# Three edits in an attention, expert and gated-unit kernel: no zeroing of x2, splits moved in the queues, a narrower low product

## The chip, the cores and the metric

The kernel runs on one core of one Trainium2 chip. The metric is device time in microseconds. The kernel before took 451.92 us (median of three runs, 451.65 to 452.31). The engines are TensorE (PE, with its weight load PEld), VectorE (DVE), ScalarE (ACT), GpSimd (POOL) and SyncE (SP, which issues most DMAs).

## The reference, cut to what matters

Three parts follow on each other. A linear attention with a decayed state runs over 768 tokens of 2 batches and 8 heads of 48, which gives 1536 tokens of 384 values. A layer of eight experts sends each token to the one with the highest gate value. A gated unit follows:

```
h   = maximum(disp @ w1, 0)          # per expert, 384 -> 1024
y   = h @ w2                         # 1024 -> 384
x   = gate_w * y, back in the tokens' order
out = (silu(x @ w_gate) * (x @ w_val)) @ w_out   # 384 -> 1536 -> 384
```

All is in float32. The kernel reaches that precision with fp32r matmuls, by splitting each operand in a high and a low part (the cast to fp32r, and what the cast left over) and adding three products: high by high, high by low, low by high.

## The kernel before, in words

The attention takes the first 77 us. It is not touched. Its last step gives the experts' inputs: the rows of x lie in DRAM sorted by expert, each expert's block has room for 224 tokens (BLK), and x2 (three tiles of 128 rows by 1536 + 224 columns, in SBUF) takes the experts' results, one column for each token in the order of the experts.

**An expert** (`experts`, loop over e, then over f from 0 to 15) has an up phase (f below 8) and a down phase. In the up phase each f does nine matmuls of 224 columns (line 857): for each of three slices k of the input the high weights by the high part of x, by its low part, and the low weights by the high part. The first expert uses plain float32 there (line 869). `relu` then makes the high part (ScalarE, 876) and the low part (VectorE, 877) of the hidden values, side by side in one tile of 448 columns, high in the first 224 (HI) and low in the others (LO). In the down phase each f does three calls of `product`, one for each k: the high weights by all 448 columns (line 846), and the low weights by the first columns (line 847). `store` adds the two halves of the result and writes them to x2 at the expert's place (896, 897). Several experts' blocks overlap in x2: each writes 224 columns from its first token on, and the next one writes over what was too much.

Beside this the loop splits weights for later (`feed`: a cast on ScalarE, line 713, and a subtraction on VectorE, 714), loads weights (703), turns the next expert's rows by TensorE (838), and splits them in the high part (`x_part`: ScalarE, 729) and the low part (VectorE, 730), one k for each f behind the turn. In the first expert the turn is at f = 11, the parts at f = 12 to 14; four memsets at f = 8 to 11 (1020) zero x2's first 1536 columns, 384 at a time, between the first expert's weight splits.

**The gated unit** (`gated`) works on four groups g of 384 tokens, and on six chunks c of 256 hidden values, of which the first three go chunk by chunk over all groups. `inner(c, g)` has two steps f; each does 18 matmuls of 384 columns (gate and value, lines 1072 to 1074), then Silu on ScalarE (1076), the product on VectorE (1077), the cast of the high part on ScalarE (1080) and the subtraction on GpSimd (1081). `outer` does the last product (1094 to 1096) for the group before. `x2_split` splits x2 for one group and one k (ScalarE 1044, VectorE 1045). Groups 0 and 1 are split while the last expert runs; the six splits of groups 2 and 3 are in the list `later`, of which one is taken in each of the first six steps. `background` does a step of the conversion of the gated unit's weights in between (790 to 823).

Nothing is scheduled by a planner: the order within each engine's queue is that in which the code issues the instructions, each engine takes its queue in order, and semaphores hold an instruction until its inputs are there and its output's buffer is free.

Of the kernel before, what the change touches and what calls it, by code (L numbers as in the profile page):

```python
# [41 lines left out]
HI, LO = slice(0, BLK), slice(BLK, 2 * BLK)  # L42
# [10 lines left out]
TG = 384  # L53
# [16 lines left out]
class Kernel:  # L70
# [772 lines left out]
    def product(self, ps, wh, wl, xc, first, last):  # L843

        nc = self.nc
        nc.tensor.matmul(ps[:, 0:2 * BLK], lhsT=wh, rhs=xc, start=first, stop=False, skip_group_check=True)  # L846
        nc.tensor.matmul(ps[:, 0:256], lhsT=wl, rhs=xc[:, 0:256], start=False, stop=last, skip_group_check=True)  # L847

    def up(self, f, x):

# [78 lines left out]
    def experts(self, st):  # L929
        tc, nc, a, cp = self.tc, self.nc, self.a, self.cp  # L930
        hpool = self.ep = self.pool(st, "ep", side="right")
        self.ps_y = self.pool(st, "ps_y", space=PSUM)
        self.ps_x = self.pool(st, "ps_x", space=PSUM)
        x2 = self.x2

        NU = 8
        by_f = [(f, k) for f in range(NF) for k in range(KD)]
        by_k = by_f[0:KD * NF // 2] + [(f, k) for k in range(KD) for f in range(NF // 2, NF)]


        counts = self.counts
        offs = self.offs = cp.tile([P, E], F32, name="offs")
        self.by_expert = cp.tile([P, NT], I32, name="by_expert")
        offs_i = cp.tile([1, 2, E], I32, name="offs_i")
        rare = cp.tile([P, 2], F32, name="rare")
        rare_i = self.rare_i = cp.tile([1, 1], I32, name="rare_i")

        def order():
            self.order()
            nc.vector.tensor_copy(offs_i[:, 0], offs[0:1])  # L950
            for e in range(1, E):
                nc.vector.tensor_scalar(
                    out=offs_i[:, 1, e:e + 1], in0=counts[0:1, e:e + 1], scalar1=float(e * ST), scalar2=None, op0=ALU.add
                )

            nc.vector.tensor_reduce(rare[:, 0:1], counts, AX.X, ALU.max)
            nc.vector.tensor_scalar(out=rare[:, 0:1], in0=rare[:, 0:1], scalar1=float(BLK), scalar2=None, op0=ALU.is_gt)
            nc.vector.scalar_tensor_tensor(
                out=rare_i, in0=self.bad[0:1], scalar=float(HP * (P - 2 * D)), in1=rare[0:1, 0:1],
                op0=ALU.is_gt, op1=ALU.add,  # L960
            )


        n_loaded, n_split = RAWS, 1

        def feed(used):

            nonlocal n_split
            if n_split < min(max(used - 4, 0) + WS, E * NU - 4):
                self.unit_split((n_split + 4) % NU)  # L970
                n_split += 1

        def load(n, used, eng=None):
            nonlocal n_loaded
            for _ in range(n):

                o = n_loaded - RAWS
                if n_loaded < E * NU and (o < used if o < 4 else o - 4 < n_split):
                    self.unit_load(n_loaded // NU, n_loaded % NU, eng)
                    n_loaded += 1  # L980

        x = self.x0
        last, xrs = None, {}
        for e in range(E):
            hc, py = self.tiles()
            for f in range(2 * NF):
                if f < NF:
                    ph = self.up(f, x) if e else self.up_plain(f, x)
                else:

                    i = (f - NF) * KD
                    self.down((by_f if e + 1 < E else by_k)[i:i + KD], py, hc)
                if e == 0 and f == 1:
                    xrs[1] = self.x_block(ST)
                if f == (5 if e == 0 else 1):
                    if e == 0:
                        self.places()
                    if e + 2 < E:

                        end = nc.values_load(  # L1000
                            offs_i[0:1, 1, e + 2:e + 3], engines=[ET.SP], min_val=(e + 2) * ST, max_val=(e + 2) * ST + N
                        )
                        self.clear_rows(self.x_disp[ds(end, BLK)])
                    if e == 0:
                        self.background(1, 2)
                if e == 1 and f < NT:
                    self.place_id(f)
                turn = NF + 2 if e else NF + 3
                if f == turn and e + 1 < E:
                    x = self.new_x(self.x_turn(xrs[e + 1]))  # L1010
                if turn < f <= turn + KD and e + 1 < E:
                    self.x_part(x, f - turn - 1)
                if f % 2:
                    feed(e * NU + f // 2)

                load(2, e * NU + (f + 1) // 2, nc.scalar if e == 0 and f < 4 else None)
                if f == NF + 5 and e + 2 < E:
                    xrs[e + 2] = self.x_block((e + 2) * ST)
                if e == 0 and f in range(8, 12):
                    nc.vector.memset(x2[:, :, (f - 8) * TG:(f - 7) * TG], 0.0)  # L1020
                if f in ((12, 14) if 0 < e < E - 3 else (10, 12, 14) if 0 < e < E - 1 else ()):
                    self.background(1, 2)
                if f < NF:
                    self.relu(f, ph, hc)
                if e == 0 and f == 3:
                    order()
                if last and f in (0, 2, 4):
                    self.store(*last, f // 2)
                if e == E - 1 and NF <= f < NF + 2 * KD:
                    self.x2_split((f - NF) // KD, [(f - NF) % KD])  # L1030
                if e == E - 1 and f >= 2 * NF - KD:
                    self.store(py, self.place(offs_i[0:1, 0, e:e + 1], ET.DVE), f - (2 * NF - KD))
            for q in range(0 if e else 4, NU):
                self.units[q].pop(0)
            if e < E - 1:
                last = py, self.place(offs_i[0:1, 0, e:e + 1], ET.DVE)
# [10 lines left out]
    def gated(self, st, at_end=lambda: None):  # L1047
        nc, a = self.nc, self.a
# [10 lines left out]
        later = []  # L1059

        def inner(c, g, steps, limit):

            parts = []
            xh, xl = self.x2s[g]
            for f in range(2):
                pg = {}
                fs = slice(f * P, (f + 1) * P)
                for m in ("w_gate", "w_val"):
                    wh, wl = self.wff[c % 3][m]
                    pg[m] = (pg2.tile([P, 512], F32, name="g2", tag="g2") if f else self.pa_tile())[:, 0:TG]  # L1070
                    for k in range(KD):
                        nc.tensor.matmul(pg[m], lhsT=wh[:, k, fs], rhs=xh[:, k], start=(k == 0), stop=False)
                        nc.tensor.matmul(pg[m], lhsT=wh[:, k, fs], rhs=xl[:, k], start=False, stop=False)
                        nc.tensor.matmul(pg[m], lhsT=wl[:, k, fs], rhs=xh[:, k], start=False, stop=(k == KD - 1))  # L1074
                sg = wk.tile([P, TG], F32, name="sg", tag="sg", bufs=3)
                nc.scalar.activation(sg, pg["w_gate"], AF.Silu)  # L1076
                nc.vector.tensor_mul(sg, pg["w_val"], sg)  # L1077
                h_ = wk.tile([P, TG], F32R, name="ah", tag="ah", bufs=8)
                l_ = wk.tile([P, TG], F32R, name="al", tag="al", bufs=8)
                nc.scalar.copy(h_, sg)  # L1080
                nc.gpsimd.tensor_sub(l_, sg, h_.bitcast(F32))  # L1081
                parts.append((h_, l_))
                if later:
                    self.x2_split(*later.pop(0))
                self.background(steps, *limit)
            return [(c, f, *parts[f]) for f in range(2)]

# [27 lines left out]
        for c in range(HALF):  # L1115
            for g in range(NG):

                limit = (c + 3, True) if g else (c + 2, False)
                parts = inner(c, g, 2 if c else 1, limit)
                if before:  # L1120
                    outer(*before, False, 1, limit)
                before = g, parts, c == 0
# [157 lines left out]
```

## Time and profile before

| | |
|---|---|
| median of three runs | 451.92 us (451.65 to 452.31) |
| profiled execution | 451.35 us |
| its span, first to last instruction | 449.7 us |
| TensorE busy | 430.9 us (96%) |
| VectorE, ScalarE, GpSimd busy | 293.5, 213.2, 156.6 us |
| mean granted TensorE clock | 0.989 of full speed |
| experts | about 77 to 213 us |
| gated unit | about 213 to 440 us |

The profile is of one execution. A row of the timeline gives the start and the duration in microseconds, the engine, the line, the operation and the tiles it writes and reads; in brackets stands how long the engine had been idle just before, and which instruction ended that. Matmuls overlap in the pipeline, so what one of them costs is read from the distance of two starts, not from its duration. Weight loads run beside the matmuls.

### The profile page before, as it was taken

To read this page: it belongs to the slowest core of one execution; us is meant where nothing else is said; L and a number is where in the kernel's file an instruction comes from. 1 tells how busy PE (TensorE), PEld (TensorE's weight loads), DVE (VectorE), ACT (ScalarE), POOL (GpSimd) and SP (SyncE) were. 2 spreads that over 40 slices of the span, in tenths; PEclk is the share of its full clock that TensorE was granted. 3 is DMA by queue.
4 is the path that set the end of the run, shared out by engine and by line. 5 is a ranking of instruction groups with operands and counts; after the bars stand their busy time and mean duration, and the time that the engine had idled before them with its cause. 6 is when DMAs were issued, how large, how long until landed. Compare 5 with 4: busy or idle time off the path is not lost. (4 is left out here: it accounts for less than half of the span.)

```text
span 449.7 us, 8371 instructions
## 1 busy us (share of the span) xinstructions
PE 430.9 (96%) x3179; PEld 417.5 (93%) x3179; DVE 293.5 (65%) x576; ACT 213.2 (47%) x471; POOL 156.6 (35%) x147
## 2 busy tenths in 40 slices
PE   8889989999999999999999999999999999999991
PEld 7778778989999999999998999999999999999991
DVE  6999985886887977986557788978865111111110
ACT  2688864636756756755555534353343031230310
POOL 5846543102111110000343556454546233332321
PEclk9999999989999999999999999999999999999996
DMA  7999932698999999602022423233200100101001
GB/s 260 355 303 354 404 107 78 204 369 251 265 224 254 279 261 256 231 1 72 0 71 70 136 85 133 79 133 111 101 1 1 52 1 17 37 0 54 1 20 41
DMA packets 24819, 63.78 MB, mean 142 GB/s; under 512 B 4801, under 2 KB 10049, under 8 KB 24769
## 3 DMA queue, kind: packets, MB, share of 16 engines
q1 hardware_dynamic: 22128, 57.43, 40.1%
q0 software_dynamic: 1920, 4.73, 2.9%
q10 hardware_dynamic: 720, 1.00, 0.8%
q8 instruction: 27, 0.44, 0.4%
q14 instruction: 24, 0.19, 0.1%
HBM read 55.67 MB, written 7.48 MB: 140 GB/s over the span
## 5 line engine op out<-in xcount | busy, mean ns | idle before, releaser
L1081 POOL TENSOR_TENSOR al<-sg,ah 128x384 fp32r<-128x384 f32 x48 | 54.2, 1128 | 135.2 <-ACT ah L1080 135.2
L714 DVE TENSOR_TENSOR wlo<-raw,whi 128x768 fp32r<-128x768 f32 x60 | 57.3, 954 | 9.3 <-ACT whi L713 9.1
L846 PE MATMUL py<-hc,whi 128*128 128x448 f32 x192 | 63.1, 370 | 0.0
L1080 ACT CAST ah<-sg 128x384 fp32r<-128x384 f32 x48 | 24.7, 515 | 78.2 <-DVE sg L1077 78.2
L857 PE MATMUL A<-xc,whi 128*128 128x224 f32 x336 | 59.2, 280 | 1.0 <-DVE xc L730 0.9
L857 PEld LDWEIGHTS A<-xc,whi 128*128 128x128 f32 x336 | 52.5, 196 | 1.9 <-DVE xc L730 1.5
L847 PE MATMUL py<-hc,wlo 128*128 128x256 f32 x192 | 53.8, 280 | 0.0
L713 ACT CAST whi<-raw 128x768 fp32r<-128x768 f32 x60 | 49.8, 837 | 0.7 <-PE py L846 0.7
L1094 PE MATMUL po<-w_out_hi,ah 128*128 128x384 f32 x144 | 48.6, 337 | 0.0
L1096 PE MATMUL po<-w_out_hi,al 128*128 128x384 f32 x144 | 48.5, 337 | 0.0
L1095 PE MATMUL po<-w_out_lo,ah 128*128 128x384 f32 x144 | 48.5, 337 | 0.0
L857 PE MATMUL A<-xc,wlo 128*128 128x224 f32 x168 | 46.9, 279 | 0.0
L924 POOL DMA_INDIRECT ids<-tok,by_expert x12 | 13.7, 1145 | 75.6 <-DMA ids<-tok,by_expert 67.2
L1103 DVE TENSOR_TENSOR acc<-acc,po 128x384 f32<-128x384 f32 x36 | 19.3, 547 | 30.9 <-PE po L1096 30.9
L846 PEld LDWEIGHTS py<-hc,whi 128*128 128x128 f32 x192 | 36.1, 188 | 2.5
L1077 DVE TENSOR_TENSOR sg<-A,sg 128x384 f32<-128x384 f32 x24 | 13.3, 555 | 38.0 <-PE A L1074 30.3
L847 PEld LDWEIGHTS py<-hc,wlo 128*128 128x128 f32 x192 | 36.5, 190 | 0.0
L1077 DVE TENSOR_TENSOR sg<-g,sg 128x384 f32<-128x384 f32 x24 | 13.3, 555 | 34.5 <-PE g L1074 27.6
L876 ACT ACTIVATE hc<-A 128x224 fp32r<-128x224 f32 x64 | 23.1, 362 | 22.8 <-PE A L857 20.0
L276 ACT ACTIVATE AT<-ident,c 128x128 f32<-128x128 f32 x96 | 29.4, 389 | 9.6 <-DVE c L263 9.6
L857 PEld LDWEIGHTS A<-xc,wlo 128*128 128x128 f32 x168 | 33.1, 197 | 0.0
L1076 ACT ACTIVATE sg<-A 128x384 f32<-128x384 f32 x24 | 11.6, 485 | 34.7 <-PE A L1074 34.7
(169 smaller groups left out, 1100.7 us busy)
## 6 DMA issues: line engine op xcount, KB each, us to landing
raw<-in_w SPq DMA_DIRECT2D x62, 384.0 KB, 6.8
rkT<-in_rkT SPq DMA_DIRECT2D x12, 512.0 KB, 6.5
rk<-in_rk SPq DMA_DIRECT2D x12, 384.0 KB, 4.7
raw<-in_w_gate SPq DMA_DIRECT2D x6, 768.0 KB, 4.2
raw<-in_w_val SPq DMA_DIRECT2D x6, 768.0 KB, 4.1
raw<-in_w_out SPq DMA_DIRECT2D x6, 768.0 KB, 4.3
x_disp<-zero SPq DMA_DIRECT2D x8, 336.0 KB, 8.1
xr<-x_disp SPq DMA_DIRECT2D x8, 336.0 KB, 6.1
```

The lines of the kernel that those rows point to most:

```text
L276: nc.scalar.activation(AT[i][:, j, hp], ident, AF.Copy, scale=cc[i][:, j, hp:hp + 1])
L713: nc.scalar.copy(h_, raw)
L714: nc.vector.tensor_sub(l_, raw, h_.bitcast(F32))
L846: nc.tensor.matmul(ps[:, 0:2 * BLK], lhsT=wh, rhs=xc, start=first, stop=False, skip_group_check=True)
L847: nc.tensor.matmul(ps[:, 0:256], lhsT=wl, rhs=xc[:, 0:256], start=False, stop=last, skip_group_check=True)
L857: self.nc.tensor.matmul(ph[:, HI], lhsT=w[:, k, fs], rhs=x[1][:, k, half], start=(k == 0 and i == 0), stop=(k == KD - 1 and i == 2),)
L1077: nc.vector.tensor_mul(sg, pg["w_val"], sg)
L1080: nc.scalar.copy(h_, sg)
L1081: nc.gpsimd.tensor_sub(l_, sg, h_.bitcast(F32))
L1094: nc.tensor.matmul(po, lhsT=ah[:, ts_], rhs=wh, start=(i == 0), stop=False)
L1095: nc.tensor.matmul(po, lhsT=ah[:, ts_], rhs=wl, start=False, stop=False)
L1096: nc.tensor.matmul(po, lhsT=al[:, ts_], rhs=wh, start=False, stop=(i == len(parts) - 1))
```

## The change

x2 is no longer zeroed. In the gated unit a step's split from the list `later` is issued ahead of the step's matmuls, where it was issued behind the step's casts. In the experts' down product the low weights take the 224 columns of the high part, where they took 256 (the last 32 of these were columns of the low part).

```diff
@@ product
         nc.tensor.matmul(ps[:, 0:2 * BLK], lhsT=wh, rhs=xc, start=first, stop=False, skip_group_check=True)
-        nc.tensor.matmul(ps[:, 0:256], lhsT=wl, rhs=xc[:, 0:256], start=False, stop=last, skip_group_check=True)
+        nc.tensor.matmul(ps[:, HI], lhsT=wl, rhs=xc[:, HI], start=False, stop=last, skip_group_check=True)
@@ experts
                     xrs[e + 2] = self.x_block((e + 2) * ST)
-                if e == 0 and f in range(8, 12):
-                    nc.vector.memset(x2[:, :, (f - 8) * TG:(f - 7) * TG], 0.0)
                 if f in ((12, 14) if 0 < e < E - 3 else (10, 12, 14) if 0 < e < E - 1 else ()):
@@ gated, inner
             for f in range(2):
                 pg = {}
+                if later:
+                    self.x2_split(*later.pop(0))
                 fs = slice(f * P, (f + 1) * P)
...
                 parts.append((h_, l_))
-                if later:
-                    self.x2_split(*later.pop(0))
                 self.background(steps, *limit)
```

## Rows read from the trace of the kernel before

**Rows 1.** The page: TensorE's busy time; its granted clock in 40 slices.
```profile
PE 430.9 (96%) x3179; PEld 417.5 (93%) x3179; DVE 293.5 (65%) x576; ACT 213.2 (47%) x471; POOL 156.6 (35%) x147
...
PEclk9999999989999999999999999999999999999996
```

**Rows 2.** Windows: stretch, length, busy PE, PEld, DVE, ACT, POOL, clock, DMA share, GB/s.
```profile
95.00:98.00 3.00, 2.01 (x10) 1.19 (x9) 2.25 (x6) 2.06 (x4) 0.45 (x1) 1.00 1.00 371
98.00:101.40 3.40, 3.40 (x17) 3.40 (x18) 2.70 (x5) 1.68 (x4) 0.00 (x0) 0.50 1.03 365
...
115.00:204.00 89.00, 89.00 (x697) 87.28 (x696) 75.52 (x136) 57.74 (x126) 9.01 (x8) 1.00 0.77 221
```

**Rows 3.** Timeline of VectorE, 88 to 98 us: start, duration, instruction, idle before.
```profile
94.14 1.02 DVE L1020 MEMSET x<- 128x1152 f32 x1 [0.19 <-issue]
95.07 0.33 DVE L730 TENSOR_TENSOR xc<-px,xc 128x224 fp32r<-128x224 f32 x1
...
97.42 0.38 DVE L730 TENSOR_TENSOR xc<-px,xc 128x224 fp32r<-128x224 f32 x1
```

**Rows 4.** Timeline of TensorE, 97 to 110 us.
```profile
97.86 0.45 PE L857 MATMUL A<-xc,whi 128*128 128x224 f32 x1 [0.68 <-DVE xc L730]
```

**Rows 5.** Timeline of ScalarE, 88 to 98 us.
```profile
91.34 0.35 ACT L729 CAST xc<-px 128x224 fp32r<-128x224 f32 x1 [1.78 <-PE px L838]
95.44 0.35 ACT L729 CAST xc<-px 128x224 fp32r<-128x224 f32 x1 [3.75 <-DVE xc L730]
```

**Rows 6.** Groups by line, VectorE, 86 to 97 us: busy, mean ns, idle before.
```profile
L1020 DVE MEMSET x<- 128x1152 f32 x4 | 4.1, 1018 | 0.8 <-issue 0.8
```

**Rows 7.** Timeline of TensorE, 120 to 128 us: up product, then down product.
```profile
119.74 0.28 PE L857 MATMUL A<-xc,wlo 128*128 128x224 f32 x1
...
123.09 0.27 PE L857 MATMUL A<-xc,wlo 128*128 128x224 f32 x1
...
123.41 0.28 PE L847 MATMUL py<-hc,wlo 128*128 128x256 f32 x1
...
125.98 0.28 PE L847 MATMUL py<-hc,wlo 128*128 128x256 f32 x1
```

**Rows 8.** Window of line 857 alone: length, busy PE, PEld, clock, DMA share, GB/s.
```profile
95.00:101.47 6.47, 5.47 (x24) 4.66 (x25) 0.74 1.01 365
```

**Rows 9.** Timeline, 108 to 116 us: the next expert's start.
```profile
113.33 0.39 DVE L730 TENSOR_TENSOR xc<-px,xc 128x224 fp32r<-128x224 f32 x1
...
115.17 0.38 PE L857 MATMUL A<-xc,whi 128*128 128x224 f32 x2
```

**Rows 10.** Timeline of TensorE, 219 to 246 us, gated unit.
```profile
221.98 0.33 PE L1072 MATMUL g<-x2h,w_gate_hi 128*128 128x384 f32 x1
...
238.47 0.33 PE L1074 MATMUL A<-x2h,w_gate_lo 128*128 128x384 f32 x1
...
240.21 0.44 PE L1073 MATMUL A<-x2l,w_gate_hi 128*128 128x384 f32 x1 [0.65 <-DVE x2l L1045]
...
240.67 0.34 PE L1072 MATMUL A<-x2h,w_val_hi 128*128 128x384 f32 x1
```

**Rows 11.** Timeline of ScalarE, 205 to 246 us, gated unit.
```profile
214.47 0.49 ACT L1076 ACTIVATE sg<-A 128x384 f32<-128x384 f32 x1
...
235.17 0.51 ACT L1044 CAST x2h<-x 128x384 fp32r<-128x384 f32 x1
```

**Rows 12.** Timeline of VectorE, 205 to 246 us, gated unit.
```profile
216.01 0.56 DVE L1077 TENSOR_TENSOR sg<-A,sg 128x384 f32<-128x384 f32 x1 [2.42 <-PE A L1074]
...
219.13 0.56 DVE L1077 TENSOR_TENSOR sg<-g,sg 128x384 f32<-128x384 f32 x1 [0.50 <-PE g L1074]
...
239.10 1.05 DVE L1045 TENSOR_TENSOR x2l<-x,x2h 128x384 fp32r<-128x384 f32 x1 [0.99 <-ACT x2h L1044]
```

**Rows 13.** Timeline of SP, and the tile raw's times to landing, 80 to 104 us.
```profile
86.73 11.13 SPq L703 DMA_DIRECT2D raw<-in_w  x10
...
DMA to landing us min/median/max: 3.7/7.5/9.2
```

## The prediction

> **What bounds the kernel now.** I read the page first: TensorE is busy 96% of the span, and the row of its granted clock shows nine tenths or more in every slice but the last [rows 1]. So time can only come from stretches where TensorE waits or runs slower, or from shorter matmuls. Next, windows by stage: from 115 to 204 us (the experts) it is busy for all 89.00 us, while VectorE and ScalarE are not full. Two narrow windows differ. In 95 to 98 us it is busy for 2.01 of 3.00 us, and in 98 to 101.4 us it is busy throughout, but with a granted clock of 0.50, which is the level of 1.2 GHz instead of 2.4 [rows 2]. The average in the page's slices hides both. The third view is the timeline around the waits, and the fourth the spacing of the matmuls in the experts' two products.
>
> The stall at 95 us is the start of the second expert. Its first up product needs the three low parts of x (line 730, VectorE). They are made at 95.07 to 97.42 us [rows 3], and TensorE's eighth matmul waits for the last of them until 97.86 us [rows 4]. VectorE was late because it came from the zeroing of x2: the fourth memset runs at 94.14 us and the first part of x starts as it ends, although ScalarE's high part had been there since 91.34 + 0.35 = 91.69 us [rows 3, 5].
>
> **x2 is not zeroed.** It removes four memsets of 1.02 us, with 0.8 us of idle time before them that no engine is blamed for: 4.1 + 0.8 = 4.9 us of VectorE's queue between 88 and 95.2 us [rows 6]. Without them line 730 could start at 95.07 - 4.9 = 90.2 us by its own queue; what is late next is ScalarE's cast, at 91.69 us. From there I keep the spacing of the chain (ScalarE's second cast waits for VectorE's first part, then a weight split, then the third part): the third part ended 97.42 + 0.38 - 95.07 = 2.73 us after the first one began [rows 3], so now at 91.7 + 2.73 = 94.4 us. TensorE wants it seven matmuls after its start at 95.0 us. An undisturbed up product takes 3.35 us for 30 matmuls (119.74 to 123.09 us), 111.7 ns each [rows 7], so it is wanted at 95.8 us, with 1.4 us to spare. The stall goes.
>
> Its price: in the 6.47 us from 95.0 to 101.47 us TensorE did 24 matmuls of this product [rows 4, 8]. At 111.7 ns they take 2.68 us, so 3.79 us are lost. Of these 97.86 - (95.0 + 7 x 0.1117) = 2.08 us are waiting, and the 17 matmuls from 97.86 us on lose 3.61 - 1.90 = 1.71 us, nearly all of it to the half clock. TensorE's clock fell right behind the only stretch since the experts began in which it waited, so I count the fall as a part of the stall: **3.79 us**, between 0 (something else holds the chain) and 3.79. The next expert's start is no new stall: there the last part begins at 113.33 us, and the up product at 115.17 us [rows 9], and no memset lies in it.
>
> **The low product with 224 columns.** It is issued 192 times, all in the experts, where TensorE sets the pace. A pair (448 columns with the high weights, 256 with the low) takes 2.57 us / 8 = 321 ns (123.41 to 125.98 us) [rows 7]. Pure columns: 32 of 704 would be 14.6 ns a pair, 2.8 us in all. That is the upper end. But matmuls of 224 columns run at 111.7 ns apiece, and the 256's share of the pair is 321 x 256 / 704 = 117 ns, so a 224 that costs what it costs in the up product gains 5 ns: 192 x 5 = **1.0 us**. The lower end is the place where a 224 with low weights already stands before a 448: 123.09 to 123.41 us, 0.32 us [rows 7], the same as a pair of now, which would be a gain of 0. It cannot be a loss, since the same weights are loaded and fewer columns stream. I take 1.0, because the 30 matmuls resolve nanoseconds and the single step does not.
>
> A rule of the Trainium skill speaks against this edit: "TensorE: Matmul & The Clock Gate", section "LDWEIGHTS (loading the stationary operand)", prices a weight load by its columns, by its formula 107 ns for 128 columns. By it a low matmul could not shrink under 107 ns, however few its columns, since each next matmul brings other weights; the gain would be 117 - 107 = 10 ns a pair, 1.9 us, and the forecast 444.7 us (an estimate from that page). The trace's 111.7 ns for 224 columns, which is longer than columns alone would give, fits a floor near there.
>
> **The later splits ahead of the matmuls.** Six splits (a cast on ScalarE, a subtraction on VectorE) move in both queues from behind a step's own Silu, product and casts to ahead of its Silu. Nothing is added, and no DMA moves: SP and GpSimd keep their order. Now the last split is cast late, and its subtraction starts at 239.10 us; TensorE waits for it until 240.21 us [rows 10, 12]. From 238.47 to 240.67 us four matmuls start [rows 10]; the 95 before, from 221.98 us on, took 16.49 us, 173.6 ns each, so 2.20 - 0.69 = **1.51 us** are lost. In the new order the last cast comes where the split before it stood or earlier, about 235.2 us [rows 11], its subtraction is over by about 237, and it is wanted at 238.6. The stall goes, with 1.6 us to spare. Bounds 0 to 1.51.
>
> What is queued behind a moved split is the step's Silu on ScalarE and its product on VectorE. Both wait for the step's matmuls, 9 of them for the Silu and 18 for the product (3.1 us), and that hides 0.51 us of cast and 1.05 us of subtraction [rows 10 to 12]. In the first step the Silu, at 214.47 us, would end 0.51 us later, at 215.47, and the product starts at 216.01 us anyway [rows 11, 12]. If that cover failed, TensorE would notice when it wants a PSUM buffer back: the second step's is free at 219.13 + 0.56 = 219.69 us and wanted at 221.98 us [rows 10, 12], so 2.29 us of delay cost nothing.
>
> **Sum.** 3.79 + 0.98 + 1.51 = 6.28 us. The profiled execution took 451.35 us (span 449.7 and 1.65 around it), which gives 445.07. The median of the runs is 0.57 us above the profiled one, so I predict **445.6 us**.
>
> **Rivals.**
> 1. *The clock falls all the same*, at another place or for a shorter wait that stays at the second expert's start. For it: the fall followed on about 2 us of waiting, and how little would do, no row shows. Against it: the chain has 1.4 us to spare. It costs the 1.71 us again: 447.3 us. Chance 0.10.
> 2. *Another thing holds the chain at 95 us.* ScalarE's next cast, at 95.44 us, waits for VectorE [rows 5], so the two go in turns, and a weight load could take the memsets' place: loads issued from 86.73 us on land in 3.7 to 9.2 us, so until 95.9 us [rows 13]. Against it: the split in the chain reads an earlier load, and no row shows ScalarE waiting for one. The 3.79 us stay: 449.4 us. Chance 0.06.
> 3. *The splits ahead do nothing*, because the two engines stay as late as they are: 1.51 us back, 447.1 us. Chance 0.05.
> 4. *Slower: the splits get into the chain from matmul to Silu to product.* If each of the six puts 0.51 + 1.05 = 1.56 us in front of its product, that is 9.4 us; less the 2.29 us that the PSUM buffers allow, TensorE waits 7.1 us, and one fall of the clock like that at 98 us adds 1.71. Against the 4.77 us that the other edits bring, it ends 4.0 us slower, 455.9 us. It decides once a product is over 2.29 us late. For it: products do run late here, as the splits do. Against it: the product at 219.13 us waited for TensorE (0.50 us idle), not for its own queue [rows 12]. Chance 0.05.
>
> **How the numbers follow.** The forecast has 0.74. Its own range goes from a full 2.8 us on the low product (443.8 us) to none (446.6 us). To leave out no more than 2 in 10 I go on to the first and third rival: 443.8 to 447.4 us. About 0.2% (0.9 us) is what a measurement of this kernel tells from no change. Faster takes the forecast and the first three rivals, 0.95, less a little for several misses together: 0.94. Slower is the fourth, 0.04 after the same rounding, and 0.02 are left for no difference.
>
> **What would show it.** No memset, and the third low part of x over by 94.5 us, with the second expert's matmuls 112 ns apart from the first on; a granted clock of 1.00 up to the last matmul (the first edit). 316 ns a pair against 321, or 307 if columns alone count, and no change in the up product (the second). No wait of TensorE in the fourth group of the gated unit, and the last subtraction ahead of 237 us on the old scale (the third). The forecast is wrong if TensorE still waits at the second expert's start, if the clock falls anywhere ahead of the end, or if TensorE waits for a PSUM buffer in the gated unit's first three groups.

## The result, and the profile after

The changed kernel took 445.89 us (median of six executions, 445.19 to 447.7) against 452.12 us before; the ratio is 0.9861, with a 95% interval of 0.9832 to 0.9891. Its profiled execution took 446.19 us, with a span of 444.5 us where before had 449.7.

The page after: TensorE's row, and its granted clock in 40 slices. They answer to [rows 1].

```profile
PE 426.2 (96%) x3179; PEld 414.0 (93%) x3179; DVE 289.0 (65%) x572; ACT 213.4 (48%) x471; POOL 157.5 (35%) x147
...
PEclk9999999999999999999999999999999999999997
```

VectorE has four instructions fewer (572 for 576). The page alone doesn't tell where the time went, so I read windows cut at the same instructions in both kernels: the first expert's down product, the second expert up to the third's first matmul, the six experts behind it, and the gated unit. Columns: stretch, its length, busy time of PE, PEld, DVE, ACT and POOL, granted clock, DMA share, GB/s. Before:

```profile
86.54:95.01 8.47, 8.47 (x57) 8.12 (x55) 7.71 (x11) 2.55 (x5) 1.75 (x2) 1.00 0.99 329
95.01:115.17 20.16, 19.17 (x128) 18.00 (x127) 14.74 (x29) 12.95 (x27) 2.78 (x3) 0.92 0.93 266
115.17:212.61 97.44, 97.44 (x752) 95.39 (x751) 80.44 (x146) 61.62 (x136) 9.01 (x8) 1.00 0.74 210
212.61:439.93 227.32, 226.35 (x1297) 225.79 (x1296) 117.16 (x151) 79.58 (x147) 98.61 (x75) 1.00 0.16 55
```

After:

```profile
87.79:96.11 8.32, 8.32 (x57) 7.97 (x55) 6.44 (x12) 4.71 (x9) 1.74 (x2) 1.00 0.99 320
96.11:112.33 16.22, 16.22 (x129) 15.84 (x127) 12.10 (x24) 10.80 (x23) 2.37 (x3) 1.00 1.02 335
112.33:209.03 96.70, 96.70 (x753) 94.51 (x751) 80.22 (x146) 61.64 (x136) 10.11 (x8) 1.00 0.74 212
209.03:434.76 225.73, 225.73 (x1297) 225.73 (x1296) 116.54 (x151) 79.77 (x147) 98.66 (x75) 1.00 0.16 55
```

The four stages give 0.15, 3.94, 0.74 and 1.59 us, 6.42 us together. TensorE is now busy for the whole of all four; before, it was idle for 0.99 us of the second and 0.97 us of the fourth. Idle time is less than time lost: a matmul of the up product lasts 0.27 us, but where nothing is in the way the next one starts 0.11 us behind it. So a wait is priced here by the length of its stage. The spans differ by less than the stages, 5.2 us, because what lies ahead of the four, the attention and the first expert's up product, which the change doesn't touch, ended 1.25 us later in this execution (87.79 for 86.54 us).

The start of the second expert after, by the timelines of VectorE, ScalarE and TensorE (start, duration, instruction, idle before), answers to [rows 3 to 5]:

```profile
92.89 0.39 DVE L730 TENSOR_TENSOR xc<-px,xc 128x224 fp32r<-128x224 f32 x1 [1.13 <-ACT xc L729]
...
95.31 0.38 DVE L730 TENSOR_TENSOR xc<-px,xc 128x224 fp32r<-128x224 f32 x1
```

```profile
92.51 0.35 ACT L729 CAST xc<-px 128x224 fp32r<-128x224 f32 x1 [1.74 <-PE px L838]
93.32 0.35 ACT L729 CAST xc<-px 128x224 fp32r<-128x224 f32 x1 [0.46 <-DVE xc L730]
...
94.81 0.84 ACT L713 CAST whi<-raw 128x768 fp32r<-128x768 f32 x1 [0.16 <-DMA raw<-in_w]
```

```profile
92.84 0.27 PE L847 MATMUL py<-hc,wlo 128*128 128x224 f32 x1
...
95.37 0.27 PE L847 MATMUL py<-hc,wlo 128*128 128x224 f32 x1
...
96.11 0.39 PE L857 MATMUL A<-xc,whi 128*128 128x224 f32 x2
96.33 0.27 PE L857 MATMUL A<-xc,wlo 128*128 128x224 f32 x1
96.44 0.38 PE L857 MATMUL A<-xc,whi 128*128 128x224 f32 x2
```

VectorE now waits for ScalarE (1.13 us) instead of the other way round, the third low part is over at 95.69 us, and the up product runs at full pace from its first matmul. It is wanted seven matmuls after 96.11 us, at 96.89, so 1.2 us are to spare. A weight split's cast waits 0.16 us for its load, which the second rival had named, but it lies behind the last cast of this chain and holds nothing up. The eight pairs from 92.84 to 95.37 us take 2.53 / 8 = 316 ns, where [rows 7] gave 321.

The gated unit after, by the timelines of VectorE and TensorE, answers to [rows 10, 12]:

```profile
230.32 1.16 DVE L1043 TENSOR_TENSOR x2l<-x,x2h 128x384 fp32r<-128x384 f32 x1
231.41 0.55 DVE L1077 TENSOR_TENSOR sg<-g,sg 128x384 f32<-128x384 f32 x1
```

```profile
234.02 0.34 PE L1072 MATMUL A<-x2h,w_gate_hi 128*128 128x384 f32 x1
...
235.07 0.34 PE L1072 MATMUL A<-x2h,w_gate_hi 128*128 128x384 f32 x1
235.24 0.34 PE L1073 MATMUL A<-x2l,w_gate_hi 128*128 128x384 f32 x1
```

The last split is over at 231.48 us and is first used at 235.07 us, 3.6 us later; nothing stands in brackets behind the matmuls.

### The profile page after: what moved, and what is told of

It is laid out like the page before. It is cut to its first block, busy times and chain, and to the rows that moved or that the text cites. A ratio compares the mean times of both kernels' runs of the same rounds, so it can differ in the third digit from the quotient of the medians.

```text
span 444.5 us, 8371 instructions
## 1 busy us (share of the span) xinstructions
PE 426.2 (96%) x3179; PEld 414.0 (93%) x3179; DVE 289.0 (65%) x572; ACT 213.4 (48%) x471; POOL 157.5 (35%) x147
## 5 line engine op out<-in xcount | busy, mean ns | idle before, releaser
L846 PE MATMUL py<-hc,whi 128*128 128x448 f32 x192 | 62.2, 378 | 0.0
L857 PE MATMUL A<-xc,whi 128*128 128x224 f32 x336 | 56.7, 274 | 0.0
L847 PE MATMUL py<-hc,wlo 128*128 128x224 f32 x192 | 51.4, 268 | 0.0
L857 PEld LDWEIGHTS A<-xc,whi 128*128 128x128 f32 x336 | 51.0, 192 | 0.1
L1092 PE MATMUL po<-w_out_hi,ah 128*128 128x384 f32 x144 | 48.6, 337 | 0.0
```

Source lines behind the costliest of these rows:

```text
L847: nc.tensor.matmul(ps[:, HI], lhsT=wl, rhs=xc[:, HI], start=False, stop=last, skip_group_check=True)
L857: self.nc.tensor.matmul(ph[:, HI], lhsT=w[:, k, fs], rhs=x[1][:, k, half], start=(k == 0 and i == 0), stop=(k == KD - 1 and i == 2),)
L1092: nc.tensor.matmul(po, lhsT=ah[:, ts_], rhs=wh, start=(i == 0), stop=False)
```

## The experiments

Times of whole executions scatter by about as much as two of the three edits bring, so each experiment is read by its stages, in windows as above, and by the time where it resolves anything. Each diff is against the kernel before.

**The three edits one by one.** Without the zeroing (e1):

```diff
-                if e == 0 and f in range(8, 12):
-                    nc.vector.memset(x2[:, :, (f - 8) * TG:(f - 7) * TG], 0.0)
```

> The kernel before, without the four memsets of x2 and nothing else changed. Theory (VectorE's queue makes the low parts of x late, TensorE waits, and its clock falls behind that wait): the second expert, from its first up matmul to the third expert's, shrinks from 20.16 us to about 16.4 us, no wait at its start, granted clock 1.00 up to the last matmul, 448.1 us in all (3.8 us less). Rival 1, the clock falls without that wait too: 18.1 us for the second expert, 449.8 us. Rival 2, another thing holds the chain (a weight load or ScalarE): 20.2 us, 451.9 us.

The low product alone (e2):

```diff
-        nc.tensor.matmul(ps[:, 0:256], lhsT=wl, rhs=xc[:, 0:256], start=False, ...)
+        nc.tensor.matmul(ps[:, 0:224], lhsT=wl, rhs=xc[:, 0:224], start=False, ...)
```

> The kernel before with 224 columns in place of 256 in the low product alone. Theory (a 224-column matmul costs what it costs in the up product, 112 ns): pairs at 316 ns, six experts from the third on 0.7 to 0.8 us shorter than the 97.44 us of before, 450.9 to 451.1 us in all, with the wait at the second expert's start still there and a little longer. Rival, columns alone count: pairs at 307 ns, 2.1 us less for the six experts, 449.1 us. Rival, no gain at all: pairs at 321 ns.

The splits alone (e3):

```diff
                 pg = {}
+                if later:
+                    self.x2_split(*later.pop(0))
...
-                if later:
-                    self.x2_split(*later.pop(0))
                 self.background(steps, *limit)
```

> The kernel before with the later splits ahead of their step's matmuls, nothing else changed. Theory: the gated unit, from its first to its last matmul, shrinks from 227.32 us to about 225.8 us because TensorE no longer waits for the last split; 450.4 us in all. Rival, the two engines stay as late: 227.3 us. Rival, the splits hold up Silu and product: TensorE waits for a PSUM buffer in the first three groups, above 227.5 us.

And the zeroing kept, but issued on GpSimd (e4):

```diff
-                    nc.vector.memset(x2[:, :, (f - 8) * TG:(f - 7) * TG], 0.0)
+                    nc.gpsimd.memset(x2[:, :, (f - 8) * TG:(f - 7) * TG], 0.0)
```

> The kernel before with the four memsets issued on GpSimd in place of VectorE, so that x2 is zeroed at the same places in the order. Theory (only VectorE's queue matters): the second expert as without the memsets, about 16.4 us, 448.1 us in all. Rival, the zeroing itself costs (its writes, or GpSimd's work slowing VectorE beside it): between 16.4 and 20.2 us, with line 730's and 714's instructions longer than the 0.38 and 0.95 us of before.

Ran beside each other on one chip, where the kernel before took 450.66 us (31 executions):

| | median us | ratio, 95% interval |
|---|---|---|
| e1, no zeroing | 448.59 | 0.9945 (0.992 to 0.9971) |
| e2, 224 columns | 450.42 | 0.9991 (0.997 to 1.0012) |
| e3, splits ahead | 449.14 | 0.9984 (0.9954 to 1.0014) |
| e4, zeroing on GpSimd | 448.62 | 0.9943 (0.9914 to 0.9972) |

The time alone resolves only the zeroing. The windows resolve all. The second expert of e1:

```profile
95.37:111.70 16.33, 16.33 (x128) 15.97 (x127) 12.33 (x24) 10.80 (x23) 2.13 (x3) 1.00 1.02 331
```

The second expert and the six behind it in e2:

```profile
94.86:114.99 20.13, 19.01 (x128) 17.84 (x127) 14.71 (x29) 12.95 (x27) 2.40 (x3) 0.92 0.95 269
114.99:211.70 96.71, 96.71 (x752) 94.52 (x751) 80.20 (x146) 61.65 (x136) 10.36 (x8) 1.00 0.73 212
```

The second expert and the gated unit of e3, and a stretch of its attention:

```profile
98.11:116.63 18.52, 17.55 (x129) 16.38 (x127) 14.58 (x29) 12.84 (x27) 2.28 (x3) 1.00 1.00 300
214.06:439.79 225.73, 225.73 (x1298) 225.73 (x1296) 117.37 (x151) 79.68 (x147) 97.74 (x75) 1.00 0.16 55
48.60:55.50 6.90, 6.90 (x68) 5.85 (x67) 5.10 (x15) 4.79 (x15) 5.21 (x6) 0.51 1.03 407
```

The second expert of e4:

```profile
97.61:113.94 16.33, 16.33 (x128) 15.99 (x127) 12.32 (x24) 10.79 (x23) 2.10 (x3) 1.00 1.02 337
```

e1 is as forecast by stage: 20.16 goes to 16.33 us, TensorE busy throughout. Its time is not: 3.8 us less were forecast, the medians show 2.1, and the interval of the ratio allows 1.3 to 3.6. e4 falls short in the same way (3.8 forecast, 2.0 by the medians). e3, below, shows why. e2 takes 0.73 us off the six experts as forecast and leaves the wait. e3 takes 1.59 us off the gated unit, and its TensorE waits for no buffer there. e4 is like e1 with the zeroing done, so what cost the time was the place in VectorE's queue. The four memsets ran from 80.52 us on there, right behind the last scatter, when GpSimd had nothing to do; so e4 says nothing about a memset that runs on GpSimd beside VectorE's chain.

e3 brought what I had not expected. Its second expert still has the wait (TensorE busy for 17.55 of 18.52 us), but the clock stayed at 1.00 and the stage took 18.52, not 20.16 us. So the wait alone costs 18.52 - 16.33 = 2.19 us, and the fall of the clock, where it comes, 1.64 more (20.16 - 18.52). The 3.83 us between before and e1 were the two together, in an execution that had both. In e3's execution the clock had fallen in the attention instead (0.51 from 48.6 to 55.5 us), in code that no edit touches.

**How much of VectorE's queue is too much.** Two, three and six memsets in place of four (e5, e6, e10). Each of these three, and of e7 and e8 further on, was executed once, so they are read by their stages alone:

```diff
-                if e == 0 and f in range(8, 12):
+                if e == 0 and f in (8, 9):          # e6: (8, 9, 10); e10: range(8, 12), those at 8 and 9 twice
```

> The kernel before with two of the four memsets of x2 (those at f = 8 and 9; the later half of x2 isn't zeroed). Theory (VectorE's queue): the third low part comes 2.45 us earlier than the 97.80 us of before, 95.35 us, and is wanted at 95.8 us, so TensorE does not wait; second expert 16.4 us as without any memset. Rival, each memset costs its share of the 3.8 us: 18.2 us.

> The kernel before with three of the four memsets of x2 (f = 8 to 10; the last quarter of x2 isn't zeroed). Theory: the third low part comes at 96.6 us on the scale of before and is wanted at 95.8 us, so TensorE waits about 0.85 us there; second expert 17.2 us if the clock stays, up to 18.9 us if it falls behind this shorter wait. Rival, each memset costs its share: 19.2 us.

> The kernel before with six memsets in place of four (those at f = 8 and 9 issued twice). Theory (VectorE's queue, 1.21 us for each memset that is over the spare time): the wait at the second expert's start is 2.18 + 2.42 = 4.6 us, second expert 20.95 us with the clock at 1.00 there, and 1.65 us more, 22.6 us, for each fall of the clock that follows. Rival, something else takes over as the limit: under 20 us.

The second expert of e5:

```profile
95.17:111.50 16.33, 16.33 (x129) 15.99 (x128) 13.10 (x26) 11.15 (x24) 3.31 (x3) 1.00 1.04 328
```

The same of e6:

```profile
94.96:112.33 17.37, 16.69 (x128) 16.15 (x127) 13.91 (x27) 12.13 (x26) 2.69 (x3) 1.00 1.03 312
```

The same of e10, and the stretch in it where the clock was low:

```profile
95.05:118.72 23.67, 20.31 (x128) 19.13 (x127) 17.33 (x31) 13.04 (x27) 5.28 (x4) 0.86 0.89 238
99.05:105.87 6.82, 6.33 (x28) 5.95 (x29) 4.45 (x8) 3.49 (x10) 0.96 (x1) 0.50 0.78 195
```

Its TensorE timeline, the matmul that waited for the third low part:

```profile
100.55 0.56 PE L857 MATMUL A<-xc,whi 128*128 128x224 f32 x1 [0.49 <-DVE xc L730]
```

With the clock at 1.00, the stage takes 16.33, 16.33, 17.37 and 18.52 us for 0, 2, 3 and 4 memsets. The first two are free, each one more costs 1.04 and 1.15 us, near the 1.21 us that a memset holds the queue (1.02, and the 0.19 in front of it). So the chain has some 2.6 us to spare (3 x 1.21 - 1.04, or 4 x 1.21 - 2.19), and only what lies over it is paid for. Each memset paying its share (18.2 us for e5) is out. e10 lies at 23.67 us: 20.95 by the theory, and 2.72 us more for a clock that was low for 6.82 us. I had named 1.65 us for each fall; the low stretch was twice as long as that in [rows 2], and it began while the chain was still late: TensorE was held for the third low part until 100.55 us. Half of the 5.32 us behind that is 2.66, close to the 2.72. So the direction held, and the price of one fall did not carry over to a longer one.

**Where the columns stop paying.** 192 and 128 columns with the low weights (e7, e8). These leave out a part of the result, as the expectations say.

```diff
-        nc.tensor.matmul(ps[:, 0:256], lhsT=wl, rhs=xc[:, 0:256], start=False, ...)
+        nc.tensor.matmul(ps[:, 0:192], lhsT=wl, rhs=xc[:, 0:192], start=False, ...)   # e8: 128
```

> The kernel before with 192 columns in the low product (of 256; the last 32 of the 224 results lack their part from the low weights). Theory (a floor of 112 ns for each matmul that brings new weights, whatever its columns): pairs at 316 ns as with 224 columns. Rival, columns alone: 321 x 640 / 704 = 292 ns. Rival, a floor at 107 ns: 311 ns.

> The kernel before with 128 columns in the low product (of 256; the last 96 of the 224 results lack their part from the low weights). Theory (the floor): pairs still at 316 ns. Rival, columns alone: 321 x 576 / 704 = 263 ns. Rival, a floor at 107 ns: 311 ns.

The six experts of e7:

```profile
113.58:210.34 96.76, 96.76 (x752) 94.29 (x751) 80.35 (x146) 61.56 (x136) 9.19 (x8) 1.00 0.74 210
```

The six experts of e8, and in a second view eight pairs of its TensorE timeline:

```profile
114.03:210.34 96.31, 96.31 (x753) 94.13 (x751) 80.21 (x146) 61.59 (x136) 9.54 (x8) 1.00 0.73 212
```

```profile
122.32 0.22 PE L847 MATMUL py<-hc,wlo 128*128 128x128 f32 x1
122.38 0.42 PE L846 MATMUL py<-hc,whi 128*128 128x448 f32 x1
122.63 0.22 PE L847 MATMUL py<-hc,wlo 128*128 128x128 f32 x1
...
124.83 0.22 PE L847 MATMUL py<-hc,wlo 128*128 128x128 f32 x1
```

The six experts hold 144 pairs. From 97.44 us, 224 columns give 0.74 us (5.1 ns a pair), 192 give 0.68 (4.7 ns) and 128 give 1.13 (7.8 ns); columns alone would give 14.6, 29 and 58 ns. One profile each is enough for that: in the eight profiles with 256 columns this stage takes 97.43 to 97.55 us, and in the three with 224 it takes 96.70 to 96.73. So nearly all that can be had is there at 224 columns, at about 316 ns a pair: 192 columns bring nothing more, and 128 bring 0.4 us, 2.7 ns a pair (2.51 us / 8 = 314 ns by the second view). That is no sharp floor, and it lies between the 316 ns of the theory and the 311 of the rival. Columns alone and no gain at all are out. The single starts mislead here: in e8 the high matmul starts 60 ns behind the low one and the next low one 250 ns behind that, where it was 120 and 210 before. What the low matmul saves stands partly in the distance behind its neighbour. Only the sum over the pair is read.

**The changed kernel and the one before once more** (e9, e11).

> The changed kernel again, against the kernel before on one chip. Theory A (the fall of the clock is a part of the wait at the second expert's start, in each execution): 3.8 + 0.9 + 1.55 = 6.3 us less, a ratio of 0.986. Theory B (formed from three profiles with the same wait and no fall: the fall follows it in some executions only; the wait alone costs 2.18 us): 2.18 + 0.87 + 1.55 = 4.6 us less where the mean clock of both is 0.991 or more, 445.4 us against 450.0, a ratio between 0.9885 and 0.990 over all. Second expert 16.2 us, six experts 96.7 us, gated unit 225.7 us by both.

> The kernel before once more, for its profile. Theory B (the fall follows the wait in some executions only): second expert 18.5 us without a fall behind the wait or 20.2 us with one; 13 of 31 executions of it so far show a mean clock under 0.991, so 18.5 us is the likelier. Theory A (always): 20.2 us.

The second expert, the six behind it and the gated unit in e9:

```profile
95.57:111.77 16.20, 16.20 (x129) 15.85 (x127) 12.43 (x24) 10.80 (x23) 3.41 (x3) 1.00 1.03 322
111.77:208.50 96.73, 96.73 (x753) 94.52 (x751) 80.23 (x146) 61.58 (x136) 8.48 (x8) 1.00 0.76 213
208.50:434.23 225.73, 225.73 (x1297) 225.73 (x1296) 117.36 (x151) 79.64 (x147) 97.71 (x75) 1.00 0.16 55
```

The second expert of e11:

```profile
95.45:113.96 18.51, 17.52 (x128) 16.36 (x127) 14.58 (x29) 12.86 (x27) 2.49 (x3) 1.00 1.02 294
```

The same stage in e7 and in e8, which have the four memsets too:

```profile
95.06:113.58 18.52, 17.42 (x129) 16.18 (x127) 14.64 (x29) 12.84 (x27) 2.75 (x3) 1.00 1.01 304
95.52:114.03 18.51, 17.33 (x129) 16.15 (x127) 14.69 (x29) 12.84 (x27) 2.65 (x3) 1.00 1.01 293
```

e9 took 445.69 us against 451.48 us, a ratio of 0.9894 (0.986 to 0.9927). The three stages repeat those of the first profile of the change within 0.03 us. The kernel before (e11) took 18.51 us for its second expert at a clock of 1.00, where its first profile took 20.16. Six profiles have all four memsets on VectorE ahead of that wait: the first one, e2, e3, e7, e8 and e11. The wait is in all six; the clock fell behind it in two, the first one and e2. So theory A, the fall as a part of the wait in each execution, is out. By theory B the executions at like clocks should differ by 4.6 us: the seven of each kernel in e9 with a mean clock of 0.991 or more have medians of 445.5 and 450.57 us, 5.1 us apart, nearer to B's 4.6 than to A's 6.3. B's 4.6 us (0.990) lies well inside the ratio's interval, and A's 0.986 at its end. The times alone would not decide it: the first comparison, 0.9861, lies on A's value. The profiles do.

## Why the prediction was right, and where not

**The zeroing: the mechanism and the wait right, the clock wrong.** The wait was put at 2.08 us and is 2.18 to 2.19 (18.51 or 18.52 less 16.33). It is VectorE's queue, by e1 and e4, and the third low part came 1.2 us ahead of need where 1.4 was said. The step that failed is "I count the fall as a part of the stall: **3.79 us**". It was right for the execution profiled (20.16 - 16.33 = 3.83), but one profile was taken for all executions, and the fall can also come where nothing was changed, as in e3's attention. What the zeroing brings is 2.2 us in every execution profiled and 1.65 more in those where the clock fell behind the wait. One row was misread on the way: the granted clock in [rows 1] is not nine tenths or more in every slice but the last. Its ninth slice, 90 to 101 us, shows eight, which is this fall, so the page did not hide it. And by the prediction's own sign, a clock that falls anywhere ahead of the end, its first rival seems to have come true in some executions: the slowest of the six of the changed kernel, 447.7 us, has a mean clock of 0.988, where the other five have 0.992 or more. Where in it the clock fell is not on record.

**The low product.** 1.0 us was forecast, from the up product's 111.7 ns as a floor. Measured: 0.15 us in the first expert, 0.74 in the six, and 16.33 - 16.22 = 0.11 in the second, 1.00 together. The upper end (2.8 us, columns alone) and the lower one (none) are both out, by the stages of e2, e7 and e8. From the price of a weight load in the Trainium skill's "TensorE: Matmul & The Clock Gate", section "LDWEIGHTS (loading the stationary operand)", the prediction had worked out another floor, an estimate of 107 ns with a gain of 1.9 us. The trace agrees that fewer columns soon bring next to nothing, but the gain was 1.00 us and not 1.9, and the measurement decides. Where the floor lies below 224 columns stays open, since e8's pairs come out between the two, and a pair divides into its two matmuls only by an assumption. That the weight load itself makes the floor is argued, not shown; no run here took the load away.

**The splits.** 1.51 us forecast, 1.59 measured, in e3 alone and in the change. The last split came earlier than I had said: 235.1 us on the scale of before (231.48 + 3.58, the distance between the two gated units' starts), not 237. I had moved only that one split and left the queue behind it as late as it was. But before, VectorE sat idle for 0.99 us between each product and its split, as in [rows 12], because the cast in front stood behind another that needed that product. In the new order the first, the fourth and the last split have no idle time in front of them, and the sixth product starts at 231.41 us, 234.99 on the scale of before, where it was 237.57. The other three splits still wait for their casts (1.73, 1.31 and 2.00 us), so it is the chain that got shorter and not all waiting that went. The fourth rival, the splits in the way of Silu and product, is out: no wait of TensorE in the gated unit.

**The sum.** 6.28 us were forecast and the stages of the two profiles give 6.42, but that they agree is in part luck, since the profile of before held a fall of the clock behind the wait and other executions do not. The change itself is worth 4.8 us of the sum in the stages at a clock of 1.00 (2.2 + 1.0 + 1.6), and up to 6.4 where the clock fell in the kernel before. The two comparisons, 0.9861 and 0.9894, lie at the two ends of that, and their intervals overlap (0.986 to 0.9891). The absolute 445.6 us, close to 445.89 and to the 445.69 us of e9, is on firmer ground: it takes the fall out of an execution that had it. From e11's execution, 450.42 us without that fall, the same three terms with the wait alone (2.19 + 0.98 + 1.51) would have led to 445.74 us.

## What to carry to other kernels

Read a wait's cost by the stage it lies in, cut at the same instructions in both kernels, and where a fall of TensorE's clock stands behind it, look at more than one profile before you add the fall to the wait. Work on a side engine is free up to the spare time of the chain that it delays, and each instruction above that costs nearly its full length: find that spare time, and then move the work to an engine that is idle (here GpSimd) or leave it out. Fewer columns need not make a matmul shorter: here, where each brings new weights, almost all of the gain was there at 224, so look for the number from which fewer bring next to nothing, and read it from sums over whole groups, since single starts push what is saved onto the neighbour.

## What the runs showed of the hardware that was not expected

The clock's fall is not tied to the wait alone. With the same four memsets and the same 2.2 us of waiting it came in two of six profiles; of the two of the very same kernel, the first had it and e11 did not. In e3 and e4 it came in the attention. There, too, TensorE had been partly idle just before, but a stretch as idle in another execution brought no fall. From 46 to 48 us in e3, where the fall followed, and in e9, where none did:

```profile
46.00:48.00 2.00, 0.85 (x17) 0.64 (x13) 1.93 (x6) 2.00 (x6) 0.24 (x2) 1.00 1.05 410
46.00:48.00 2.00, 0.87 (x16) 0.65 (x12) 1.97 (x5) 1.87 (x6) 0.26 (x2) 1.00 0.98 372
```

From 24 to 26 us in e4, with the fall that followed, and in the first profile of the change, without one:

```profile
24.00:26.00 2.00, 1.16 (x15) 1.02 (x17) 1.82 (x4) 2.00 (x8) 1.47 (x2) 0.98 1.03 388
25.90:29.30 3.40, 3.40 (x40) 2.91 (x42) 3.11 (x6) 2.92 (x10) 0.62 (x2) 0.50 1.00 362
```

```profile
24.00:26.00 2.00, 1.14 (x8) 0.97 (x8) 1.97 (x4) 2.00 (x8) 1.29 (x2) 1.00 1.06 414
```

Over whole executions a mean clock under 0.991 came in 29 of 65 with the four memsets on VectorE (before in the comparisons of e1 to e4 and of e9, e2, e3) and in 10 of 35 without (the changed kernel twice, e1, e4). That doesn't settle whether the wait makes a fall more frequent, and a mean doesn't say where the clock fell. What decides it in one execution stays open: no run here set it on and off.

A split's subtraction of 128 by 384 values on VectorE took 0.56 us with GpSimd idle beside it and 2.08 us while GpSimd worked on the weights. VectorE's timeline after, and GpSimd's:

```profile
214.72 0.56 DVE L1043 TENSOR_TENSOR x2l<-x,x2h 128x384 fp32r<-128x384 f32 x1 [1.73 <-ACT x2h L1042]
...
217.89 2.08 DVE L1043 TENSOR_TENSOR x2l<-x,x2h 128x384 fp32r<-128x384 f32 x1 [1.31 <-ACT x2h L1042]
```

```profile
217.71 1.85 POOL L823 TENSOR_TENSOR w_out_lo<-mag,w_out_hi 128x768 fp32r<-128x768 f32 x1
```

The move of the splits put this one beside that instruction; in e3 it took 2.07 us there. In the kernel before, an instruction of line 792 lay there, with 2.20 us where the median of its 18 is 0.55:

```profile
221.67 2.20 DVE L792 TENSOR_SCALAR bits<-raw 128x768 int32<-128x768 int32 x1
```

```profile
221.29 2.16 POOL L823 TENSOR_TENSOR w_out_lo<-mag,w_out_hi 128x768 fp32r<-128x768 f32 x1
```

No run took GpSimd's instruction away, so that it is the cause is read from the overlap alone. TensorE did not wait for the split in the end, but such a meeting is what moving an instruction in a queue can bring about.
